# A reordered step table and one copy on another engine, in a fused attention and MLP kernel

## The chip, the cores and the metric

The kernel runs on one NeuronCore of a Trainium2 chip. Its time is the device time of one execution in microseconds (us). Five engines work beside each other, each through its own queue in order: TensorE (PE; its weight loads are shown as PEld), VectorE (DVE), ScalarE (ACT), GpSimd (POOL) and SyncE (SP). DMAs are issued from POOL, SP and ACT, and are carried by 16 DMA engines.

## The reference

Linear attention with decay (4 batches, 8 heads, 768 tokens, head size 64) and behind it an MLP with the activation h + sin(alpha h)^2 / alpha (512 to 2048 to 512). Cut to what is computed:

```python
for b in range(nb):                                   # blocks of 64 tokens
    intra = einsum('bhic,bhjc->bhij', qb, kb) * Dmask
    intra = einsum('bhij,bhjd->bhid', intra, vb)
    inter = einsum('bhid,bhde->bhie', qb * lam_pow, kv_state)
    out[:, :, sl] = intra + inter
    kv_state = lam_block * kv_state + einsum('bhsd,bhse->bhde', kb * rev_pow, vb)
x = out.transpose(0, 2, 1, 3).reshape(B * S, H * D)   # 3072 x 512
h = x @ w_in
s = sin(alpha * h)
g = h + s * s / (alpha + 1e-09)
return g @ w_out
```

## The kernel before

**Tiling.** The 768 tokens are cut into six chunks of 128 (t or g = 0 to 5); a chunk holds these tokens of all four batches, 512 columns. Per chunk the attention gives xt, 512 features x 512 tokens, and the MLP then runs over 16 blocks f of 128 hidden features and, for the output, over four batches m. Matmuls are bf16 into PSUM, which has eight banks of 128 x 512 f32.

**Order.** The first chunk's attention and the tables are written out in plain code. All that follows is one table, the string `ORDER` at the top: 652 words, each a step, issued in exactly this order by the loop at the end through the dictionary `STEP`. An engine runs its own steps in the table's order; between engines only data and buffers make it wait. `h1.4:7` is step h for chunk 1, block 4, in PSUM bank 7. The letters:

- TensorE: `h` the hidden block (four matmuls of 512 columns, L325), `u g.m.part` a quarter of the output projection (four matmuls, L352; part p needs blocks 4p to 4p+3 finished), `F` scores for two batches (four banks, L256), `K` new state from k and v (two banks, L276), `O` attention output (carried part L297, inside part L304, four banks), `e` the last projection in two pieces, 384 and 128 columns (L368).
- ScalarE: `s` sine out of the h bank (L330), `q` its square (L336), `B` cast of the state (L289), `o` copy of an output bank, with the store issued from SP (L358, L360).
- VectorE: `t` finish, which reads the square and the h bank, writes gall and so frees the bank (L345); `Q` and `P` are the square on VectorE, as a tensor_tensor (L338) or a scalar_tensor_tensor (L340); `m` mask of scores (L262), `x` scaling of the attention output (L313), `k` and `j` the transposes of raw k and raw q (L246), `S` the state's update (L285; on ScalarE for chunk 0).
- GpSimd: `I`, `W` loads of w_in and w_out, `r`, `R` of raw k and raw q (four issues each, L123), `n`, `v` of k and v as they lie (two issues each, L130), `d` the decay of k in place (L267), `C` a cast of the state.

A block's chain is thus h, s, q (or Q, P), t, and then the bank is free. Raw k and raw q have one buffer each, so r of the next chunk waits for both k steps of the last; nat_k and nat_v have two. A load from GpSimd's queue also waits until the eighth load ahead of it has landed.

**Where the change acts.** The table's stretch from chunk 1 to chunk 3 is quoted below. The copy that changes is L372 in `project_pieces`, which is the step `e`, the last word of the table:

Of the kernel before, what the change touches and what calls it, by code (L numbers as in the profile page):

```python
# [13 lines left out]


ORDER = """
s0.0 s0.1 I1 h0.4:4 h0.6:5 P0.0 P0.1 t0.0 s0.2 t0.1 s0.3 s0.4 q0.2 q0.3 q0.4 h0.7:6 I2 t0.2 t0.3 d0.1 I3 t0.4
h0.5:2 s0.5 s0.6 s0.7 P0.5 h0.11:3 t0.5 h0.9:1 W0 q0.6 q0.7 t0.6 t0.7 h0.8:0 s0.8 r1 P0.8 t0.8 h0.10:4 h0.12:2
W1 s0.9 s0.10 h0.14:6 u0.1.0:5 R1 q0.9 t0.9 q0.10 t0.10 s0.11 s0.12 h0.13:7 k1.1 u0.2.0:1 q0.11 t0.11 h0.15:4
u0.0.0:0 k1.0 q0.12 t0.12 u0.2.1 s0.13 s0.14 W2 u0.3.0:3 W3 q0.13 t0.13 s0.15 d0.0 K0:72 q0.14 t0.14 v1 u0.1.1  # L20
q0.15 t0.15 S0.0 j1.0 u0.3.1 j1.1 S0.1 F1.0:4627 C0.1 m1.0.1 u0.3.2 u0.2.2 R2 m1.0.0 m1.0.2 u0.1.2 C0.0 m1.0.3
F1.1:7462 u0.0.1 u0.1.3 o0.1 m1.1.2 u0.3.3 o0.3 m1.1.1 m1.1.3 m1.1.0 O1:7562 x1.0 x1.1 u0.0.2 u0.2.3 u0.0.3 o0.0
x1.3 x1.2 h1.0:7 h1.1:0 j2.0 r2 k2.0 h1.2:2 o0.2 s1.0 s1.1 Q1.0 t1.0 q1.1 t1.1 s1.2 h1.3:4 F2.0:6135 m2.0.2 s1.3
m2.0.1 h1.4:7 q1.2 q1.3 t1.2 n1 s1.4 m2.0.0 h1.5:0 s1.5 k2.1 m2.0.3 n2 q1.4 t1.4 h1.6:1 s1.6 q1.5 d1.1 h1.7:2
s1.7 t1.3 h1.8:6 q1.6 t1.6 h1.11:3 t1.5 s1.8 q1.7 q1.8 h1.9:5 h1.10:4 s1.9 s1.10 t1.7 t1.8 u1.0.0:1 h1.12:7 j2.1
h1.13:2 q1.9 t1.9 q1.10 s1.11 t1.10 u1.0.1 d1.0 K1:06 q1.11 t1.11 h1.14:5 u1.2.0:3 v2 S1.0 d2.1 S1.1 d2.0 K2:40
u1.2.1 s1.12 q1.12 s1.13 q1.13 h1.15:6 t1.12 t1.13 S2.0 u1.0.2 s1.14 R3 q1.14 t1.14 r3 s1.15 F2.1:4572 q1.15
S2.1 t1.15 u1.2.2 m2.1.0 B2.0 u1.1.0:0 n3 B1.0 m2.1.2 m2.1.1 B1.1 u1.0.3 u1.2.3 o1.2 B2.1 m2.1.3 O2:5672 j3.0
u1.1.1 u1.1.2 k3.0 x2.0 x2.1 o1.0 x2.3 x2.2 F3.0:4156 m3.0.0 u1.1.3 o1.1 h2.0:7 s2.0 m3.0.1 h2.1:2 k3.1 q2.0
s2.1 q2.1 j3.1 m3.0.2 h2.2:0 s2.2 v3 d3.0 u1.3.0:1 h2.3:4 u1.3.1 q2.2 t2.0 t2.1 t2.2 s2.3 d3.1 F3.1:3257 m3.1.1  # L30
m3.1.2 m3.0.3 u1.3.2 q2.3 K3:02 S3.1 h2.4:5 S3.0 m3.1.3 m3.1.0 R4 s2.4 q2.4 h2.5:6 h2.6:2 s2.5 s2.6 q2.5 t2.3
t2.5 u1.3.3 q2.6 t2.6 j4.0 r4 h2.7:0 s2.7 o1.3 h2.10:4 q2.7 t2.7 h2.8:7 s2.8 n4 O3:2613 t2.4 h2.9:0 x3.0 x3.2
h2.13:5 q2.8 s2.9 x3.3 s2.10 d4.1 d4.0 v4 v5 h2.11:2 x3.1 u2.0.0:1 q2.9 h2.12:6 t2.8 t2.9 u2.0.1 q2.10 t2.10
h3.0:3 s2.11 q2.11 t2.11 k4.0 s2.12 q2.12 t2.12 u2.0.2 s2.13 q2.13 F4.0:4207 m4.0.0 m4.0.2 t2.13 m4.0.1 B3.0
h2.14:6 s2.14 u2.3.0:4 q2.14 h2.15:0 s2.15 q2.15 u2.3.1 t2.14 k4.1 r5 h3.2:5 m4.0.3 s3.0 q3.0 t2.15 j4.1 R5 t3.0
h3.1:6 s3.1 q3.1 s3.2 h3.3:2 t3.1 u2.0.3 u2.1.0:7 q3.2 t3.2 s3.3 h3.4:0 q3.3 t3.3 u2.1.1 u2.3.2 o2.0 s3.4 q3.4
t3.4 u2.1.2 F4.1:6315 m4.1.3 B3.1 u2.3.3 o2.3 m4.1.1 u2.1.3 o2.1 m4.1.0 m4.1.2 u2.2.0:2 O4:1365 h3.5:4 s3.5
h3.6:0 x4.0 u3.1.0:7 x4.1 h3.8:1 s3.6 x4.2 q3.5 t3.5 q3.6 k5.0 h3.7:6 u2.2.1 x4.3 t3.6 s3.7 q3.7 s3.8 u3.0.0:3
u2.2.2 q3.8 h3.9:5 s3.9 q3.9 h3.10:4 s3.10 q3.10 t3.7 j5.1 j5.0 t3.8 u3.0.1 h3.11:0 K4:16 u2.2.3 t3.9 t3.10 S4.1
S4.0 s3.11 q3.11 t3.11 o2.2 u3.1.1 h3.12:1 F5.0:6042 h3.13:5 m5.0.0 u3.1.2 m5.0.3 m5.0.1 h4.0:6 h3.14:0 B4.0  # L40
s3.12 q3.12 s3.13 m5.0.2 q3.13 t3.13 t3.12 B4.1 h3.15:2 u3.2.0:1 h4.1:5 u3.2.1 u3.0.2 u3.2.2 s3.14 q3.14 s3.15
q3.15 t3.14 t3.15 u3.1.3 s4.0 q4.0 t4.0 s4.1 q4.1 o3.1 t4.1 h4.2:0 u3.0.3 o3.0 k5.1 F5.1:6542 m5.1.0 m5.1.2
h4.3:7 m5.1.3 u3.2.3 u3.3.0:6 h4.4:3 s4.2 q4.2 t4.2 m5.1.1 s4.3 q4.3 t4.3 u3.3.1 O5:4072 u3.3.2 x5.0 x5.2 x5.3
o3.2 x5.1 s4.4 q4.4 t4.4 h4.5:5 s4.5 q4.5 t4.5 u3.3.3 o3.3 h4.6:7 s4.6 q4.6 h4.8:0 t4.6 h4.7:2 s4.7 s4.8
u4.0.0:5 q4.7 t4.7 q4.8 h4.9:6 s4.9 q4.9 t4.9 h4.10:1 s4.10 h4.11:7 s4.11 q4.10 q4.11 h5.2:2 h4.12:3 s4.12 t4.8
q4.12 u4.0.1 u4.2.0:6 t4.11 h4.13:0 t4.12 h4.14:7 s4.13 q4.13 t4.13 h4.15:4 s4.14 s4.15 h5.0:3 t4.10 u4.3.0:0
s5.0 u4.0.2 q4.14 u4.2.1 q4.15 q5.0 u4.3.1 h5.1:1 s5.1 q5.1 t4.14 t4.15 u4.0.3 s5.2 q5.2 t5.0 t5.2 h5.3:4 s5.3
u4.3.2 h5.6:7 o4.0 q5.3 t5.1 u4.3.3 o4.3 h5.4:2 s5.4 q5.4 h5.5:5 s5.5 q5.5 t5.3 h5.8:3 t5.4 t5.5 s5.6 h5.7:0
s5.7 q5.6 t5.6 q5.7 s5.8 q5.8 h5.9:2 s5.9 q5.9 u4.2.2 t5.7 u5.0.0:5 u5.1.0:1 u4.2.3 o4.2 t5.9 h5.10:4 s5.10
q5.10 t5.10 h5.13:0 u5.1.1 u5.2.0:2 h5.11:6 s5.11 h5.12:4 s5.12 t5.8 q5.11 q5.12 s5.13 q5.13 t5.11 h5.14:3  # L50
u5.2.1 s5.14 h5.15:7 s5.15 q5.14 u5.2.2 u5.0.1 u5.1.2 t5.12 t5.13 t5.14 u4.1.0:4 u5.0.2 q5.15 t5.15 u5.1.3
u5.2.3 o5.1 u5.0.3 o5.0 o5.2 u4.1.1 u4.1.2 u4.1.3 o4.1 e5.3:60
"""


# [1 line left out]
def kernel(  # L57
# [304 lines left out]
    def project_pieces(g, m, *bks):  # L362
        row = m * S + g * T
        for bk, cols in zip(bks, (slice(0, 384), slice(384, DM))):
            w = cols.stop - cols.start
            ps = bank("ops", bk)
            for f in range(NFC):
                nc.tensor.matmul(out=ps[:, 0:w], lhsT=gall[g][:, f, m * P:(m + 1) * P],  # L368
                                 rhs=w_out_sb[f // 4][:, f % 4, cols],
                                 start=(f == 0), stop=(f == NFC - 1))  # L370
# [1 line left out]
            A.copy(out=o_sb[:, 0:w], in_=ps[:, 0:w])  # L372
# [182 lines left out]
```

## Time and profile before

| | |
|---|---|
| median of 3 runs | 208.8 us (208.12 to 209.15) |
| profiled execution | 207.95 us, span 206.2 |
| TensorE, share of the span | 97% |
| VectorE, ScalarE | 69%, 69% |
| GpSimd | 39%, its last load issued at 110 us |
| h and u matmuls, 368 each | 86.5 and 87.5 us |
| squares on ScalarE | 91 of 96, 55.6 us, 635 ns each |
| squares on VectorE | 4 at 687 ns (L340), 1 at 414 ns (L338) |
| masks, finishes, transposes on VectorE | 685, 741 and some 1110 ns each |
| decay of k on GpSimd | 10 at 1904 ns |

The span is the time from the first to the last event of the profiled execution; the rest of its time lies around it. A line of the profile's order of time gives start and length in us, engine, line of the kernel, operation, output and inputs, the count of instructions merged and, in brackets, the engine's idle time ahead of it and what ended it. Matmul ends are modelled and overlap the next start.

### The profile page before, as it was taken

How to read it: one execution, taken by the hardware profiler on the slowest of the kernel's cores; microseconds unless marked ns; L12 is line 12 of the kernel's file. 1: busy time of each engine (PE TensorE's matmuls, PEld its weight loads, DVE VectorE, ACT ScalarE, POOL GpSimd, SP SyncE). 2: the span in 40 equal slices, each digit the busy share in tenths (PEclk: the TensorE clock that was granted, in tenths of full speed). 3: DMA queues.
4: the chain of work that ended last, by engine and by line, in shares of the span. 5: the costliest groups of instructions: out<-in, count | busy, mean ns of one | idle time of the engine just before them, and what ended most of it. 6: DMA issues, size and time to landing. Idle time of an engine off the chain costs nothing.

```text
span 206.2 us, 4975 instructions
## 1 busy us (share of the span) xinstructions
PE 200.3 (97%) x2068; PEld 104.8 (51%) x2068; DVE 142.2 (69%) x212; ACT 142.7 (69%) x251; POOL 80.5 (39%) x103
## 2 busy tenths in 40 slices
...
GB/s 123 166 178 203 208 204 209 177 193 219 211 26 95 150 163 233 131 168 80 66 149 166 183 5 3 54 0 51 102 3 51 3 0 34 69 51 0 3 153 102
DMA packets 63808, 22.61 MB, mean 110 GB/s; under 512 B 46758, under 2 KB 60326, under 8 KB 63786
## 3 DMA queue, kind: packets, MB, share of 16 engines
...
q14 instruction: 6, 0.05, 0.1%
...
## 4 chain that ended last, share of the span: by engine, by line
PE 61%; POOL 17%; DMA 17%; issue 2%; DVE 1%; ACT 0%; POOLq 0%; DVEq 0%; ACTq 0%
PE ops L352 27%; PE hps L325 27%; POOL nat_k L267 5%; DMA nat_v<-in_v_dram 5%; DMA nat_k<-in_k_dram 5%; DMA w_out<-in_moe_w_out_dram 4%; POOL raw_q L123 3%; POOL w_in L139 3%; POOL nat_v L130 3%; DMA raw_k<-in_k_dram 3%; PE ops L368 2%; PE F_ps L256 2%; PE O_ps L304 1%; POOL nat_k L130 1%; PE O_ps L297 1%
## 5 line engine op out<-in xcount | busy, mean ns | idle before, releaser
L345 DVE SCALAR_TENSOR_TENSOR gall<-s,r_sb,hps 128x512 bf16<-128x512 bf16 x96 | 68.3, 741 | 31.2 <-ACT s L336 31.0
L352 PE MATMUL ops<-w_out,gall 128*128 128x512 bf16 x368 | 87.5, 379 | 0.0
L325 PE MATMUL hps<-xt,w_in 128*128 128x512 bf16 x368 | 86.5, 380 | 0.5 <-DVE gall L345 0.4
L330 ACT ACTIVATE s_sb<-hps,alpha_sb 128x512 bf16<-128x512 f32 x96 | 63.7, 687 | 24.3 <-PE hps L325 23.3
L325 PEld LDWEIGHTS <-w_in 128*128 128x128 bf16 x368 | 40.9, 114 | 38.0 <-issue 0.7
L336 ACT ACTIVATE s<-s_sb 128x512 bf16<-128x512 bf16 x91 | 55.6, 635 | 1.6
L352 PEld LDWEIGHTS <-gall 128*128 128x128 bf16 x368 | 35.0, 98 | 41.1
L262 DVE TENSOR_TENSOR STm<-F_ps,C 128x512 bf16<-128x512 f32 x48 | 30.3, 685 | 4.8 <-PE F_ps L256 4.6
L358 ACT COPY o_sb<-ops 128x512 f32<-128x512 f32 x23 | 13.3, 584 | 26.1 <-PE ops L352 25.9
L267 POOL TENSOR_TENSOR nat_k<-nat_k,R 128x1024 bf16<-128x1024 bf16 x10 | 18.9, 1904 | 14.3 <-DMA nat_k<-in_k_dram 14.3
L123 POOL DMA_DIRECT2D raw_q<-in_q_dram x24 | 14.2, 597 | 6.8 <-DVE turned_q L246 3.1
L313 DVE TENSOR_TENSOR xt<-O_ps,Etab 128x512 bf16<-128x512 f32 x20 | 12.5, 682 | 4.2 <-PE O_ps L304 4.2
L246 DVE STREAM_TRANSPOSE turned_q<-raw_q 128x512 f32<-128x512 f32 x12 | 12.8, 1109 | 2.1 <-DMA raw_q<-in_q_dram 1.9
L130 POOL DMA_DIRECT2D nat_v<-in_v_dram x12 | 14.0, 1174 | 0.0
L246 DVE STREAM_TRANSPOSE turned_k<-raw_k 128x512 f32<-128x512 f32 x10 | 11.2, 1116 | 3.2 <-DMA raw_k<-in_k_dram 3.2
L123 POOL DMA_DIRECT2D raw_k<-in_k_dram x20 | 11.5, 584 | 4.5 <-DVE turned_k L246 3.1
L130 POOL DMA_DIRECT2D nat_k<-in_k_dram x9 | 10.6, 1189 | 0.0
L256 PEld LDWEIGHTS <-turned_k 32*128 32x128 bf16 x384 | 6.0, 94 | 6.1 <-issue 3.1
L186 PE MATMUL spare<-fill 128*128 128x512 bf16 x18 | 7.5, 534 | 1.5 <-DVE one L167 1.5
L256 PE MATMUL F_ps<-turned_q,turned_k 32*128 32x128 bf16 x384 | 8.2, 218 | 0.3 <-DVE turned_k L246 0.2
...
L285 DVE SCALAR_TENSOR_TENSOR S<-S,L,KV_ps 128x512 f32<-128x512 f32 x8 | 5.7, 747 | 0.0
...
## 6 DMA issues: line engine op xcount, KB each, us to landing
...
```

Source lines behind the costliest of these rows:

```text
L123: (eng or G).dma_start(out=dst[quad[a], bs].rearrange("t b n r d -> t (b n) (r d)"), in_=src[t, a])
L130: G.dma_start(out=nat[nm, t][:, bs].rearrange("p b h e -> p (b h) e"), in_=SRC[nm][bs, :, t * T:(t + 1) * T, :].rearrange("b h p e -> p (b ...
L246: V.transpose(out=dst.rearrange("p (x t r) -> p x r t", r=R, t=32), in_=src.rearrange("p (x r d) -> p x r d", r=R, d=32))
L256: nc.tensor.matmul(out=F[a][:, u, n, :], lhsT=kt[:, :, e] if t else kt[:, e, :], rhs=KQ["q", t][quad[a], 2 * pr + u, n, :, e], start=(e == ...
L262: V.tensor_tensor(out=st[t, pr][:, a], in0=att["F", pr][a], in1=(C0 if t else C1)[:, a].unsqueeze(1).broadcast_to([P, 2, NQ, T]), op=ALU.mult)
L267: G.tensor_tensor(out=kd, in0=kd, in1=R128[:].unsqueeze(1).unsqueeze(3).broadcast_to([P, 2, H, D]), op=ALU.mult)
L325: nc.tensor.matmul(out=hps[g, f][:], lhsT=w_in_block(f, c), rhs=xt[g][:, c, :], start=(c == 0), stop=(c == NDC - 1))
L330: A.activation(out=s_of[g, f][:], in_=hps[g, f][:], func=ACTF.Sin, scale=alpha_sb[:, f:f + 1])
L336: A.activation(out=s2_of[g, f][:], in_=s_sb[:], func=ACTF.Square)
L345: V.scalar_tensor_tensor(out=gall[g][:, f, :], in0=s2_of.pop((g, f))[:], scalar=r_sb[:, f:f + 1], in1=hps.pop((g, f))[:], op0=ALU.mult, op ...
L352: nc.tensor.matmul(out=ops[g, m][:], lhsT=gall[g][:, f, m * P:(m + 1) * P], rhs=w_out_sb[part][:, f % 4, :], start=(f == 0), stop=(f == NF ...
L358: A.copy(out=o_sb[:], in_=ops.pop((g, m))[:])
```

## The change

Two edits. The table holds the same number of words, with loads, matmuls and banks in another order; 26 squares that were `q` are now `Q` (14 more than before) or `P` (12 more). And the second piece of the last step is copied by VectorE.

```diff
@@ project_pieces @@
-            A.copy(out=o_sb[:, 0:w], in_=ps[:, 0:w])
+            if cols.stop < DM:
+                A.copy(out=o_sb[:, 0:w], in_=ps[:, 0:w])
+            else:
+                V.tensor_copy(out=o_sb[:, 0:w], in_=ps[:, 0:w])
@@ ORDER @@
...
-u0.0.0:0 k1.0 q0.12 t0.12 u0.2.1 s0.13 s0.14 W2 u0.3.0:3 W3 q0.13 t0.13 s0.15 d0.0 K0:72 q0.14 t0.14 v1 u0.1.1
-q0.15 t0.15 S0.0 j1.0 u0.3.1 j1.1 S0.1 F1.0:4627 C0.1 m1.0.1 u0.3.2 u0.2.2 R2 m1.0.0 m1.0.2 u0.1.2 C0.0 m1.0.3
-F1.1:7462 u0.0.1 u0.1.3 o0.1 m1.1.2 u0.3.3 o0.3 m1.1.1 m1.1.3 m1.1.0 O1:7562 x1.0 x1.1 u0.0.2 u0.2.3 u0.0.3 o0.0
-x1.3 x1.2 h1.0:7 h1.1:0 j2.0 r2 k2.0 h1.2:2 o0.2 s1.0 s1.1 Q1.0 t1.0 q1.1 t1.1 s1.2 h1.3:4 F2.0:6135 m2.0.2 s1.3
-m2.0.1 h1.4:7 q1.2 q1.3 t1.2 n1 s1.4 m2.0.0 h1.5:0 s1.5 k2.1 m2.0.3 n2 q1.4 t1.4 h1.6:1 s1.6 q1.5 d1.1 h1.7:2
-s1.7 t1.3 h1.8:6 q1.6 t1.6 h1.11:3 t1.5 s1.8 q1.7 q1.8 h1.9:5 h1.10:4 s1.9 s1.10 t1.7 t1.8 u1.0.0:1 h1.12:7 j2.1
-h1.13:2 q1.9 t1.9 q1.10 s1.11 t1.10 u1.0.1 d1.0 K1:06 q1.11 t1.11 h1.14:5 u1.2.0:3 v2 S1.0 d2.1 S1.1 d2.0 K2:40
-u1.2.1 s1.12 q1.12 s1.13 q1.13 h1.15:6 t1.12 t1.13 S2.0 u1.0.2 s1.14 R3 q1.14 t1.14 r3 s1.15 F2.1:4572 q1.15
-S2.1 t1.15 u1.2.2 m2.1.0 B2.0 u1.1.0:0 n3 B1.0 m2.1.2 m2.1.1 B1.1 u1.0.3 u1.2.3 o1.2 B2.1 m2.1.3 O2:5672 j3.0
-u1.1.1 u1.1.2 k3.0 x2.0 x2.1 o1.0 x2.3 x2.2 F3.0:4156 m3.0.0 u1.1.3 o1.1 h2.0:7 s2.0 m3.0.1 h2.1:2 k3.1 q2.0
-s2.1 q2.1 j3.1 m3.0.2 h2.2:0 s2.2 v3 d3.0 u1.3.0:1 h2.3:4 u1.3.1 q2.2 t2.0 t2.1 t2.2 s2.3 d3.1 F3.1:3257 m3.1.1
-m3.1.2 m3.0.3 u1.3.2 q2.3 K3:02 S3.1 h2.4:5 S3.0 m3.1.3 m3.1.0 R4 s2.4 q2.4 h2.5:6 h2.6:2 s2.5 s2.6 q2.5 t2.3
-t2.5 u1.3.3 q2.6 t2.6 j4.0 r4 h2.7:0 s2.7 o1.3 h2.10:4 q2.7 t2.7 h2.8:7 s2.8 n4 O3:2613 t2.4 h2.9:0 x3.0 x3.2
...
+u0.0.1 m1.1.1 O1:7254 u0.0.2 u0.2.3 x1.0 x1.3 u0.0.3 r2
+o0.3 n1 n2 x1.1 x1.2 h1.0:7 v2 o0.0 h1.1:0 o0.2 h1.2:2 j2.0 j2.1 k2.0 s1.0 q1.0 s1.1 q1.1 t1.0 t1.1 h1.3:4
+F2.0:5136 d1.1 m2.0.1 h1.4:7 s1.2 s1.3 d1.0 q1.2 q1.3 m2.0.3 h1.5:0 s1.4 t1.2 s1.5 h1.6:1 s1.6 t1.3 m2.0.2
+m2.0.0 h1.7:6 q1.4 t1.4 h1.10:4 h1.8:2 q1.5 t1.5 q1.6 t1.6 s1.7 h1.9:5 h1.12:7 s1.8 d2.1 h1.11:0 k2.1 q1.7 t1.7
+s1.9 q1.8 t1.8 d2.0 q1.9 u1.0.0:1 t1.9 K1:36 S1.0 u1.0.1 s1.10 s1.11 q1.10 q1.11 t1.10 t1.11 s1.12 q1.12 h1.13:2
+s1.13 S1.1 u1.2.0:3 h1.14:5 s1.14 t1.12 K2:40 S2.0 h1.15:6 q1.13 q1.14 t1.13 t1.14 s1.15 u1.0.2 B1.1 R3 S2.1
+q1.15 t1.15 u1.2.1 B1.0 F2.1:7425 m2.1.0 u1.2.2 u1.1.0:0 u1.0.3 u1.2.3 o1.2 m2.1.2 m2.1.3 o1.0 m2.1.1 O2:6257
+j3.0 u1.1.1 u1.1.2 B2.0 r3 k3.0 x2.0 x2.1 F3.0:3216 n3 d3.1 v3 n4 u1.1.3 o1.1 x2.3 x2.2 h2.0:5 m3.0.2 h2.1:7
+m3.0.1 j3.1 u1.3.0:1 s2.0 q2.0 s2.1 h2.2:0 q2.1 k3.1 m3.0.0 s2.2 u1.3.1 t2.0 t2.1 q2.2 t2.2 h2.3:4 s2.3 q2.3
+F3.1:3257 m3.1.1 d3.0 B2.1 m3.1.2 u1.3.2 K3:02 m3.0.3 h2.4:5 s2.4 q2.4 m3.1.3 h2.5:6 m3.1.0 s2.5 t2.3 h2.8:7
+t2.4 R4 h2.6:3 S3.0 S3.1 q2.5 s2.6 u1.3.3 t2.5 h2.7:5 q2.6 t2.6 d4.0 o1.3 h2.9:0 s2.7 s2.8 j4.0 h2.10:4 q2.7
...
```

GpSimd's steps in the table, before:

```text
I1 I2 d0.1 I3 W0 r1 W1 R1 W2 W3 d0.0 v1 C0.1 R2 C0.0 r2 n1 n2 d1.1 d1.0 v2 d2.1 d2.0 R3 r3 n3 v3 d3.0 d3.1 R4 r4 n4 d4.1 d4.0 v4 v5 r5 R5
```

and after:

```text
I1 I2 d0.1 I3 W0 r1 W1 R1 W2 d0.0 W3 C0.0 v1 C0.1 R2 r2 n1 n2 v2 d1.1 d1.0 d2.1 d2.0 R3 r3 n3 d3.1 v3 n4 d3.0 R4 d4.0 r4 v4 v5 r5 d4.1 R5
```

TensorE's first steps are `h0.4 h0.6 h0.7 h0.5 h0.11 h0.9 h0.8 h0.10 h0.12 h0.14 u0.1.0` before, and `h0.4 h0.5 h0.6 h0.8 h0.7 h0.10 h0.9 h0.11 h0.12 u0.1.0` after. In chunks 4 and 5 the banks that the prediction names lie in this order on TensorE after the change: `h4.2:2 u3.1.3 h4.4:4 h4.3:3 F5.1:2507`, `h4.5:7 u3.3.1 O5:1253 h4.9:7` and `h5.0:7 u4.2.1 h5.2:2 h5.6:4 h5.3:7`; and the last words of the table are `u4.1.3 o4.1 e5.3:23` where they were `u4.1.3 o4.1 e5.3:60`.

More of the change, by code (lines that the diff above doesn't have):

```diff
@@ L16 @@
 ORDER = """
-s0.0 s0.1 I1 h0.4:4 h0.6:5 P0.0 P0.1 t0.0 s0.2 t0.1 s0.3 s0.4 q0.2 q0.3 q0.4 h0.7:6 I2 t0.2 t0.3 d0.1 I3 t0.4
-h0.5:2 s0.5 s0.6 s0.7 P0.5 h0.11:3 t0.5 h0.9:1 W0 q0.6 q0.7 t0.6 t0.7 h0.8:0 s0.8 r1 P0.8 t0.8 h0.10:4 h0.12:2
-W1 s0.9 s0.10 h0.14:6 u0.1.0:5 R1 q0.9 t0.9 q0.10 t0.10 s0.11 s0.12 h0.13:7 k1.1 u0.2.0:1 q0.11 t0.11 h0.15:4
-u0.0.0:0 k1.0 q0.12 t0.12 u0.2.1 s0.13 s0.14 W2 u0.3.0:3 W3 q0.13 t0.13 s0.15 d0.0 K0:72 q0.14 t0.14 v1 u0.1.1
-q0.15 t0.15 S0.0 j1.0 u0.3.1 j1.1 S0.1 F1.0:4627 C0.1 m1.0.1 u0.3.2 u0.2.2 R2 m1.0.0 m1.0.2 u0.1.2 C0.0 m1.0.3
@@ L32 @@
-t2.5 u1.3.3 q2.6 t2.6 j4.0 r4 h2.7:0 s2.7 o1.3 h2.10:4 q2.7 t2.7 h2.8:7 s2.8 n4 O3:2613 t2.4 h2.9:0 x3.0 x3.2
[L33 to L51, printed above, removed]
@@ L52 @@
-u5.2.3 o5.1 u5.0.3 o5.0 o5.2 u4.1.1 u4.1.2 u4.1.3 o4.1 e5.3:60
+I1 s0.0 P0.0 t0.0 I2 h0.4:7 s0.1 s0.2 P0.1 h0.5:4 s0.3 h0.6:5 h0.8:6 t0.1 h0.7:3 q0.2 P0.3 s0.4 s0.5 t0.2 t0.3
+h0.10:0 q0.4 t0.4 s0.6 q0.5 P0.6 t0.5 t0.6 h0.9:1 s0.7 s0.8 h0.11:7 d0.1 I3 h0.12:2 q0.7 t0.7 q0.8 s0.9 s0.10
+t0.8 W0 r1 u0.1.0:5 q0.9 t0.9 h0.13:4 q0.10 t0.10 k1.0 s0.11 s0.12 s0.13 W1 R1 k1.1 u0.3.0:3 q0.11 q0.12 W2
+t0.12 q0.13 t0.13 u0.2.0:1 h0.14:0 s0.14 h0.15:6 u0.2.1 s0.15 u0.1.1 t0.11 q0.14 q0.15 t0.14 t0.15 d0.0 K0:74 W3
@@ new lines @@
+S0.0 j1.0 S0.1 C0.0 v1 u0.3.1 u0.0.0:0 F1.0:7264 u0.2.2 C0.1 j1.1 m1.0.1 m1.0.2 m1.0.0 m1.0.3 u0.1.2 u0.3.2
+F1.1:7264 m1.1.3 m1.1.0 m1.1.2 u0.3.3 u0.1.3 o0.1 R2 u0.0.1 m1.1.1 O1:7254 u0.0.2 u0.2.3 x1.0 x1.3 u0.0.3 r2
+o0.3 n1 n2 x1.1 x1.2 h1.0:7 v2 o0.0 h1.1:0 o0.2 h1.2:2 j2.0 j2.1 k2.0 s1.0 q1.0 s1.1 q1.1 t1.0 t1.1 h1.3:4
+F2.0:5136 d1.1 m2.0.1 h1.4:7 s1.2 s1.3 d1.0 q1.2 q1.3 m2.0.3 h1.5:0 s1.4 t1.2 s1.5 h1.6:1 s1.6 t1.3 m2.0.2
+m2.0.0 h1.7:6 q1.4 t1.4 h1.10:4 h1.8:2 q1.5 t1.5 q1.6 t1.6 s1.7 h1.9:5 h1.12:7 s1.8 d2.1 h1.11:0 k2.1 q1.7 t1.7
@@ new lines @@
+F3.1:3257 m3.1.1 d3.0 B2.1 m3.1.2 u1.3.2 K3:02 m3.0.3 h2.4:5 s2.4 q2.4 m3.1.3 h2.5:6 m3.1.0 s2.5 t2.3 h2.8:7
+t2.4 R4 h2.6:3 S3.0 S3.1 q2.5 s2.6 u1.3.3 t2.5 h2.7:5 q2.6 t2.6 d4.0 o1.3 h2.9:0 s2.7 s2.8 j4.0 h2.10:4 q2.7
+t2.7 r4 q2.8 t2.8 O3:1263 x3.0 x3.3 s2.9 q2.9 s2.10 x3.2 q2.10 t2.10 h2.13:5 x3.1 h2.11:7 s2.11 u2.0.0:1 h2.12:6
+t2.9 q2.11 t2.11 s2.12 s2.13 k4.0 u2.0.1 h3.0:3 q2.12 t2.12 u2.0.2 F4.0:4207 m4.0.0 h2.14:6 m4.0.2 m4.0.3
+u2.3.0:4 m4.0.1 q2.13 s2.14 Q2.14 h2.15:0 t2.13 s2.15 Q2.15 t2.14 B3.0 u2.1.0:7 k4.1 h3.1:2 v4 h3.3:5 B3.1
```

17 lines of the change are left out of this document (added).

## The prediction

> **What bounds the kernel now.** I read the page first, its engine shares and slices, then TensorE's order of time, then what VectorE and GpSimd did at the places where TensorE waited.
>
> ```profile
> span 206.2 us, 4975 instructions
> PE 200.3 (97%) x2068; PEld 104.8 (51%) x2068; DVE 142.2 (69%) x212; ACT 142.7 (69%) x251; POOL 80.5 (39%) x103
> ```
>
> TensorE is busy 97% of the span, every other engine at most 69%. The change alters no matmul: both tables hold 92 h, 92 u, 10 F, 5 K and 5 O steps. So only time in which TensorE stands can be won. I price its steps by the distance from start to start where nothing waits: an h or u 0.864 us (four matmuls of 216 ns), F 0.57, K 0.62, O 1.70, and 0.10 more for whatever stands ahead of an F, K or O. From the first h at 19.82 that is 184 x 0.864 + 10 x 0.67 + 5 x 0.72 + 5 x 1.80 = 178.3, so the last step, e5.3, would start at 198.1. It starts at 199.48. **All standing in the table's part is 1.4 us**, 0.7% of the span. Nearly all of it is at two places. TensorE at the first:
>
> ```profile
> 47.95 3.62 PE L325 MATMUL hps<-xt,w_in 128*128 128x512 bf16 x16
> 51.77 0.64 PE L256 MATMUL F_ps<-turned_q,turned_k 32*128 32x128 bf16 x32 [0.20 <-DVE turned_k L246]
> 52.81 5.51 PE L325 MATMUL hps<-xt,w_in 128*128 128x512 bf16 x24 [0.39 <-DVE gall L345]
> ```
>
> Columns: start, length, engine, line, operation, tiles, count, and the wait before with what ended it. Four h from 47.95 take 3.46, plus 0.10: F2.0 was due at 51.51 and starts at 51.77, 0.27 late. h1.4 was due 0.57 later, at 52.34, and starts at 52.81, 0.46 late. The six h steps behind it lose 0.16 more (5.51 against 6 x 0.864 and 0.16 of drain). VectorE over the same time:
>
> ```profile
> 50.60 1.11 DVE L246 STREAM_TRANSPOSE turned_k<-raw_k 128x512 f32<-128x512 f32 x1 [2.31 <-DMA raw_k<-in_k_dram]
> 51.56 0.41 DVE L338 TENSOR_TENSOR s<-s_sb 128x512 bf16<-128x512 bf16 x1
> 52.01 1.41 DVE L345 SCALAR_TENSOR_TENSOR gall<-s,r_sb,hps 128x512 bf16<-128x512 bf16 x2
> 53.33 1.28 DVE L262 TENSOR_TENSOR STm<-F_ps,C 128x512 bf16<-128x512 f32 x2
> ```
>
> The transpose k2.0 stood 2.31 us for the third chunk's raw k. Queued behind it are the square Q1.0 and then t1.0, t1.1, and t1.0 frees bank 7, which h1.4 needs. The second place, TensorE and then VectorE:
>
> ```profile
> 76.88 0.90 PE L256 MATMUL F_ps<-turned_q,turned_k 32*128 32x128 bf16 x32
> 77.72 1.04 PE L352 MATMUL ops<-w_out,gall 128*128 128x512 bf16 x4
> ```
>
> ```profile
> 74.90 1.10 DVE L246 STREAM_TRANSPOSE turned_k<-raw_k 128x512 f32<-128x512 f32 x1 [0.90 <-DMA raw_k<-in_k_dram]
> 75.85 2.46 DVE L313 TENSOR_TENSOR xt<-O_ps,Etab 128x512 bf16<-128x512 f32 x4
> ```
>
> F3.0 takes 0.84 to the next step instead of 0.57: k3.0 waited for raw k until 74.77, the x2 steps came behind it, and F3.0 needs the banks that they free. That is 0.27. The rest is 0.07 ahead of O1 and six inherent 0.03s. Sum: 0.27 + 0.46 + 0.16 + 0.27 + 0.07 + 0.16 = 1.4.
>
> **The change part by part.** *h1.4 and the third chunk.* TensorE meets the same steps up to h1.6. On VectorE the order becomes j2.0 j2.1 k2.0 t1.0 t1.1: j2.1 (1.10) lies in the 2.31 us wait, and Q1.0 is gone, its square being on ScalarE (q1.0), which has t1.0's input ready before 51.5. If raw k lands at its 50.5 again, k2.0 ends at 51.7, F2.0 keeps its 0.27, t1.0 runs 51.55 to 52.3 (0.45 earlier) and h1.4, due at 52.34, no longer waits. The m steps behind end 0.46 earlier too. Removed: 0.46 + 0.16.
>
> *GpSimd from 55 us on.* Its order of time now:
>
> ```profile
> 55.41 3.76 POOL L267 TENSOR_TENSOR nat_k<-nat_k,R 128x1024 bf16<-128x1024 bf16 x2 [6.14 <-DMA nat_k<-in_k_dram]
> 59.11 2.35 POOL L130 DMA_DIRECT2D nat_v<-in_v_dram  x2
> 61.48 3.78 POOL L267 TENSOR_TENSOR nat_k<-nat_k,R 128x1024 bf16<-128x1024 bf16 x2
> 65.19 2.35 POOL L123 DMA_DIRECT2D raw_q<-in_q_dram  x4
> 67.53 2.29 POOL L123 DMA_DIRECT2D raw_k<-in_k_dram  x4
> 69.82 2.31 POOL L130 DMA_DIRECT2D nat_k<-in_k_dram  x2
> 72.11 2.30 POOL L130 DMA_DIRECT2D nat_v<-in_v_dram  x2
> 76.60 3.76 POOL L267 TENSOR_TENSOR nat_k<-nat_k,R 128x1024 bf16<-128x1024 bf16 x2 [2.19 <-DMA nat_k<-in_k_dram]
> ```
>
> v2 (the 2.35 at 59.11) goes ahead of d1.1, into the 6.14 us in which GpSimd stands. What follows d1.0 comes 2.3 us earlier: d2 59.2 to 62.95, R3 from 62.95, r3 from 65.3, n3 67.6 to 69.9. Raw k of the fourth chunk, landing 9.58 after R3's first issue as before (65.19 to 74.77), is there at 72.5, so k3.0 and x2.0, x2.1 end ahead of F3.0. Removed: 0.27. R3 needs j2.1 done, and that now ends near 49; r3 needs k2.1, near 59.7.
>
> *What is added: K3.* Before, n3 and v3 were issued back to back and d3.0, d3.1 came last. Now the order is n3 d3.1 v3 n4 d3.0 R4. d3.1 waits for n3's second half; behind it on GpSimd's queue stand v3, n4 and d3.0, and K3 on TensorE waits for v3 and d3.0. n3's issues took 6.7 and 7.4 to landing: 67.6 + 6.7 = 74.3, 68.75 + 7.4 = 76.15. Then d3.1 to 78.1, v3 to 80.35, n4 to 82.65, d3.0 to 84.55. K3 is due at 85.41 less 0.9, 84.5. v3's second half, issued at 79.2, lands 5.8 later at 85.0 if it goes like v2 at 59.11 (63.9 and 66.1), and K3's second half, due at 84.85, needs it. I take **0.3 added**, by the nearest row, v2's. The ends: nothing, and 2.3, if n3's second half lands at 78.39 as before. Then R4, some 2.8 later than before, ends close to j4.0 (both near 91.2), and t2.7 still has 0.9 before h2.13 needs bank 5.
>
> *The other moved loads.* C0.0 now stands ahead of v1, and C0.1 behind it, so v1 is issued at 36.6 instead of 32.0 and R2 perhaps 0.7 later. The DMA slices read 9 tenths through 41 us and landings follow one another (w_out's last at 40.06, v1 41.8 and 43.8), so a later issue lands the same while the line is not empty. I take nothing; 0.7 is the far end, and it would go straight onto F2.0. W3 moves behind d0.0 (1.9): it lands at 40.06 in line, its first user is due at 40.88. h0.8, the first user of the third w_in tile, goes from fifth to fourth, due at 22.41 against a landing at 22.20; u0.1.0 at 27.6 against 27.25. Nothing, at most 0.2 each.
>
> *Squares.* 26 of ScalarE's squares (635 ns each, 16.5 us, all beside TensorE) go to VectorE: 14 more as Q (414 ns) and 12 more as P (687 ns), 14.0 us. By stage VectorE was busy 16.7 of 22 us (98 to 120), 16.6 of 22, 9.2 of 14 and 15.6 of 34. With the squares, and with two transposes of 1.1 moved from the second stage to the first, these become 21.5, 18, 10.5 and 23: the first is tight. The queue there is followed step by step from these rows: the smallest spares are h5.0 to h5.3 on bank 7 (0.15), h4.2 to F5.1 on bank 2 (0.25), h4.5 to h4.9 on bank 7 (0.35). Before, h4.13 ended at 163.38 with bank 0 reused at 165.81, 2.4 later, without a wait; h5.0 to h5.3 has the same 2.4. Nothing, from -0.1 to 0.8 if several of them miss.
>
> *The last copy.* It is on the path whole:
>
> ```profile
> 202.32 0.48 ACT L372 COPY o_sb<-ops 128x384 f32<-128x384 f32 x1 [2.01 <-PE ops L368]
> 203.22 0.27 ACT L372 COPY o_sb<-ops 128x128 f32<-128x128 f32 x1 [0.41 <-PE ops L368]
> ```
>
> ScalarE has been idle 0.41 when the piece is ready, so nothing is unblocked. VectorE read 256 columns from PSUM in 425 ns and 512 in 685, a slope that gives some 295 for 128; the ends are 207 (128 columns from SBUF) and 425. Against 267 that is -0.06 to +0.16, and I take zero. [...]
>
> **Sum**: -0.62 - 0.27 + 0.3 = **-0.6 us**. The profiled execution took 207.95 with a span of 206.2, so its like would be 207.35 with 205.6. Its median over the runs is 208.8, 0.85 higher, and I carry the difference over: **208.2**.
>
> **The rivals.** *B, slower: d3.1 holds GpSimd.* If n3's second half lands at 78.39 instead of 76.15, v3, n4 and d3.0 follow at once, d3.0 ends near 86.9, and TensorE stands 2.3 us at K3: -0.9 + 2.3 = +1.4, 210.2. It turns to a loss from a landing at 77.1 on. For it: the stores o1.2 and o1.0 were under way while n3 landed, and took up to 6.6 us; v3's first half then came 4 us behind n3. Against it: n3's halves came 1.75 and 1.87 apart beside these stores, hardly slower than n2's 1.6. [...] Chance 0.17.
>
> *C, no change: the loads of the third chunk slip.* v1 and R2 are issued later, raw k lands up to 0.7 later, and F2.0 and h1.4 lose what was won: 208.8 with K3's wait at nothing. The line of DMAs without gaps speaks against it. Chance 0.13.
>
> *D, VectorE's queue.* Where squares stand ahead of a t or an m, banks come late at three or more of the places above, 0.3 to 0.8 together: 208.5 to 209.5. VectorE's spare time by stage speaks against it. Chance 0.10.
>
> **How the numbers follow.** The forecast has 0.60; its own range is 207.6 (F2.0's wait gone as well and none at K3) to 208.7. This kernel's runs, 208.12 to 209.15, tell some 0.5% from no change, about 1.0 us. More than 1.0 faster needs nearly all of the 1.4 back: 0.15. Slower by over 1.0: 0.13 of B, 0.05 of D, 0.02 of C, 0.20 together. Between: 0.65. The range runs from 207.5 to 209.9, most of the way to B.
>
> **What would show it.** Right: h1.4 starts 0.57 behind F2.0; F3.0 takes 0.57; K3 starts within 0.5 us of 84.5, d3.0 ending just ahead; the last step starts at 198.6 to 199.1. Wrong: raw k's transpose k2.0 beginning after 50.9; d3.1 beginning after 77; waits of TensorE on gall or STm beyond 100 us.

## The result, and the profile after

| | before | after |
|---|---|---|
| median of 11 runs | 208.48 us (207.81 to 209.37) | 209.59 us (209.0 to 211.12) |
| profiled execution, span | 207.95, 206.2 | 210.09, 208.4 |
| first h to e5.3, start to start | 179.66 | 182.12 |
| of it TensorE standing (less 178.28) | 1.39 | 3.84 |

The ratio after to before is 1.0062 with an interval of 1.0037 to 1.0088: the change made the kernel slower, by some 1.3 us, where 0.6 us of gain had been forecast. The direction is wrong. That the time still lies inside the range is luck: the upper end was drawn for rival B, and the larger part of the loss came from a term that was set at nothing. The profiled execution of after lies 0.5 above its median and that of before 0.5 below, so the two traces together show 2.1 us of difference, more than the medians' 1.1. The traces tell where time goes; the ratios tell how much.

The head of the page of after:

```profile
span 208.4 us, 4991 instructions
PE 199.3 (96%) x2068; PEld 104.7 (50%) x2068; DVE 153.8 (74%) x239; ACT 127.2 (61%) x224; POOL 80.5 (39%) x103
```

ScalarE is busy 15.5 us less and VectorE 11.6 more, the moved squares. TensorE's matmuls are the same 2068, and only its standing grew. Laid out step by step as in the prediction, 1.99 of the 3.84 stand at F2.0, 1.20 at K3, 0.24 at h2.13, 0.22 around F1.0, 0.11 at u2.2.0, and no other place beyond 100 us holds more than 0.03. TensorE's order of time at the first two:

```profile
47.77 3.62 PE L325 MATMUL hps<-xt,w_in 128*128 128x512 bf16 x16
53.30 0.64 PE L256 MATMUL F_ps<-turned_q,turned_k 32*128 32x128 bf16 x32 [1.92 <-DVE turned_k L246]
...
77.85 0.64 PE L256 MATMUL F_ps<-turned_q,turned_k 32*128 32x128 bf16 x32
78.42 1.04 PE L352 MATMUL ops<-w_out,gall 128*128 128x512 bf16 x4
86.11 0.42 PE L276 MATMUL KV_ps<-nat_v,nat_k 128*32 128x64 bf16 x32
87.58 0.42 PE L276 MATMUL KV_ps<-nat_v,nat_k 128*32 128x64 bf16 x32 [1.05 <-DMA nat_v<-in_v_dram]
```

F2.0 was due at 51.32 and starts at 53.30. F3.0 takes 0.57 to the next step, as forecast. K3's second half waits for the fourth chunk's v. VectorE ahead of F2.0:

```profile
47.08 2.07 DVE L246 STREAM_TRANSPOSE turned_q<-raw_q 128x512 f32<-128x512 f32 x2
52.16 1.09 DVE L246 STREAM_TRANSPOSE turned_k<-raw_k 128x512 f32<-128x512 f32 x1 [3.01 <-DMA raw_k<-in_k_dram]
53.11 0.67 DVE L345 SCALAR_TENSOR_TENSOR gall<-s,r_sb,hps 128x512 bf16<-128x512 bf16 x1
```

j2.1 lies in the wait, as planned (two transposes from 47.08), and t1.0 follows at once, without a square ahead of it. But k2.0 starts at 52.16 instead of 50.60, still waiting for raw k of the third chunk. GpSimd's order of time tells why that load is late. First before, then after:

```profile
31.99 2.37 POOL L130 DMA_DIRECT2D nat_v<-in_v_dram  x2
36.43 0.60 POOL L289 CAST Sb<-S 128x512 bf16<-128x512 f32 x1 [2.08 <-ACT S L283]
```

```profile
35.60 0.61 POOL L289 CAST Sb<-S 128x512 bf16<-128x512 f32 x1 [4.03 <-ACT S L283]
36.15 2.31 POOL L130 DMA_DIRECT2D nat_v<-in_v_dram  x2
39.00 2.30 POOL L123 DMA_DIRECT2D raw_q<-in_q_dram  x4
...
44.31 0.58 POOL L123 DMA_DIRECT2D raw_k<-in_k_dram  x1 [1.30 <-DMA nat_v<-in_v_dram]
```

C0.0 needs S0.0 from ScalarE, and GpSimd, which runs its steps in order, stood 4.03 us for it with v1 behind it. Before, v1's issues began at 31.99, ahead of both casts. The raw loads behind were issued at nearly the same times in both (the first of raw q at 38.76 and 39.00, the last of raw k at 44.12 and 44.31). From windows of 2 us, columns: stretch and length, busy time and count on PE, PEld, DVE, ACT, POOL, then granted clock, DMA share (the packets' time as a mean share of the 16 engines; packets overlap, and it passes 1 here), GB/s. First before, then after:

```profile
38.00:40.00 2.00, 2.00 (x12) 0.88 (x9) 2.00 (x4) 0.00 (x0) 1.24 (x3) 1.00 2.05 163
40.00:42.00 2.00, 2.00 (x40) 1.00 (x39) 1.18 (x3) 0.00 (x0) 2.00 (x4) 1.00 2.39 167
```

```profile
38.00:40.00 2.00, 2.00 (x11) 0.81 (x9) 2.00 (x4) 0.00 (x0) 2.00 (x4) 1.00 1.43 119
40.00:42.00 2.00, 2.00 (x40) 1.07 (x39) 1.08 (x3) 0.00 (x0) 2.00 (x5) 1.00 2.28 144
```

The DMA line ran thin: 163 GB/s became 119, 167 became 144, while the share in the thin window still reads 1.43. Over the five windows from 36 to 46 the differences (-3, 44, 23, 7 and 18 GB/s, times 2 us) come to 178 KB that had not been carried. The landings, read from the transfers: v1 itself lands within 0.2 us of before (41.64 and 44.03 against 41.82 and 43.83), but the raw loads behind it land later, the last of raw k at 52.04 instead of 50.48.

GpSimd at the second place:

```profile
60.53 3.76 POOL L267 TENSOR_TENSOR nat_k<-nat_k,R 128x1024 bf16<-128x1024 bf16 x2 [0.53 <-DMA nat_k<-in_k_dram]
...
68.84 2.34 POOL L130 DMA_DIRECT2D nat_k<-in_k_dram  x2
77.58 1.90 POOL L267 TENSOR_TENSOR nat_k<-nat_k,R 128x1024 bf16<-128x1024 bf16 x1 [6.40 <-DMA nat_k<-in_k_dram]
79.44 2.35 POOL L130 DMA_DIRECT2D nat_v<-in_v_dram  x2
81.77 2.30 POOL L130 DMA_DIRECT2D nat_k<-in_k_dram  x2
84.06 1.95 POOL L267 TENSOR_TENSOR nat_k<-nat_k,R 128x1024 bf16<-128x1024 bf16 x1
```

The same pattern: d3.1 stands 6.40 us for n3's second half (landed 77.51) and v3 stands behind it. v3's second half, issued at 80.63, lands at 87.54, and K3's second half starts at 87.58. The last copy:

```profile
205.34 0.29 DVE L375 COPY o_sb<-ops 128x128 f32<-128x128 f32 x1 [13.07 <-PE ops L368]
```

It takes 291 ns where ScalarE's took 267.

### The profile page after: what moved, and what is told of

Its sections match the earlier page's. It is cut to its first block, busy times and chain, and to the rows that moved or that the text cites. A ratio compares the mean times of both kernels' runs of the same rounds, so it can differ in the third digit from the quotient of the medians.

```text
span 208.4 us, 4991 instructions
## 1 busy us (share of the span) xinstructions
PE 199.3 (96%) x2068; PEld 104.7 (50%) x2068; DVE 153.8 (74%) x239; ACT 127.2 (61%) x224; POOL 80.5 (39%) x103
## 4 chain that ended last, share of the span: by engine, by line
PE 62%; DMA 19%; POOL 14%; issue 2%; DVE 1%; ACT 0%; POOLq 0%; DVEq 0%
PE hps L325 27%; PE ops L352 27%; DMA nat_k<-in_k_dram 8%; DMA nat_v<-in_v_dram 7%; POOL nat_k L267 5%; DMA raw_q<-in_q_dram 4%; POOL raw_q L123 3%; POOL nat_k L130 3%; PE hps L462 2%; POOL nat_v L130 2%; PE ops L368 2%; POOL raw_k L123 1%; PE F_ps L256 1%; PE O_ps L304 1%; PE O_ps L297 1%
## 5 line engine op out<-in xcount | busy, mean ns | idle before, releaser
L325 PE MATMUL hps<-xt,w_in 128*128 128x512 bf16 x368 | 86.5, 380 | 0.2 <-DVE gall L345 0.2
L325 PEld LDWEIGHTS <-w_in 128*128 128x128 bf16 x368 | 41.1, 114 | 37.2 <-issue 0.2
L336 ACT ACTIVATE s<-s_sb 128x512 bf16<-128x512 bf16 x65 | 39.8, 643 | 0.9
L123 POOL DMA_DIRECT2D raw_k<-in_k_dram x20 | 11.6, 591 | 11.8 <-DVE turned_k L246 10.2
L340 DVE SCALAR_TENSOR_TENSOR s<-s_sb 128x512 bf16<-128x512 bf16 x16 | 11.0, 686 | 1.7 <-ACT s_sb L330 1.7
L186 PE MATMUL spare<-fill 128*128 128x512 bf16 x18 | 6.9, 500 | 1.5 <-DVE one L167 1.5
```

What stands on the lines that cost most here:

```text
L123: (eng or G).dma_start(out=dst[quad[a], bs].rearrange("t b n r d -> t (b n) (r d)"), in_=src[t, a])
L325: nc.tensor.matmul(out=hps[g, f][:], lhsT=w_in_block(f, c), rhs=xt[g][:, c, :], start=(c == 0), stop=(c == NDC - 1))
L336: A.activation(out=s2_of[g, f][:], in_=s_sb[:], func=ACTF.Square)
```

## The experiments

**Theory 1** (taken up after the result): a step on GpSimd's queue that waits for another engine holds the loads behind it. C0.0 ahead of v1 costs F2.0 its 1.7 us, and d3.1 ahead of v3 costs K3 its 1.2. **Theory 2**: the loads were issued in time enough, and R2 and r2 landed late because the stores o0.1 and o0.3 ran beside them (issued at 43.30 and 43.79, landed at 50.82 and 51.77, before at 48.74 and 49.86). **Theory 3**: the squares on VectorE cost time as well. Standing is always worked out as in the table above, from the first h to e5.3. In the kernels of these runs all lines have numbers one higher (L326 for L325).

**One load back ahead of the cast** (a1_v1_first), after with

```diff
-W3 S0.0 j1.0 S0.1 C0.0 v1 u0.3.1
+W3 v1 S0.0 j1.0 S0.1 C0.0 u0.3.1
```

> The changed kernel with the two loads v1 issued right behind W3, ahead of C0.0. Theory 1 (GpSimd stands 4.0 us at C0.0 with v1 behind it, the DMA line thins near 38 us and every load of the third chunk slips): raw k of the third chunk lands near 50.5 instead of 52.04, F2.0's wait falls from 1.99 us to about 0.3, h1.4 does not wait; K3's wait stays between 0.8 and 1.5. Time about 1.6 us below the changed kernel, near 208.0, ratio to before 0.998. Theory 2 (the stores o0.1 and o0.3, issued 0.5 us apart instead of 0.86, take the DMA time from raw k): F2.0's wait stays above 1.4 us and the ratio above 1.004.

Measured: 1.0006 (0.998 to 1.0033) against before. GpSimd and one window of this kernel:

```profile
31.57 2.32 POOL L131 DMA_DIRECT2D nat_v<-in_v_dram  x2
35.63 1.16 POOL L290 CAST Sb<-S 128x512 bf16<-128x512 f32 x2 [1.75 <-ACT S L284]
```

```profile
38.00:40.00 2.00, 2.00 (x11) 0.78 (x8) 1.97 (x4) 0.00 (x0) 1.38 (x3) 1.00 2.09 162
```

The line carries as much as before again (162 GB/s against 163), raw k lands at 50.28, and F2.0 waits 0.31 instead of 1.99. The stores o0.1 and o0.3 are issued as close together as in after (at 43.23 and 43.72) and land at 48.55 and 49.55, so theory 2 falls here. K3 still stands 0.66, less than the 0.8 that was expected.

**The other load back ahead of the decay** (a2_v3_first), after with

```diff
-n3 d3.1 v3 n4
+n3 v3 d3.1 n4
```

> The changed kernel with v3 issued right behind n3, ahead of d3.1. Theory 3 (v3 is late only because it stands behind d3.1's wait for n3): v3's second half lands near 83 instead of 87.5, K3's wait falls from 1.2 us to below 0.2, and d3.0 ends earlier than 86.0 too; F2.0's wait of 2.0 stays. Time about 1.2 us below the changed kernel, near 208.4, ratio to before 1.000. Rival (K3 waits for d3.0 behind n4 anyway): K3 still waits 0.5 or more, ratio above 1.003.

Measured: 1.0007 (0.9985 to 1.0028). GpSimd and TensorE of this kernel:

```profile
68.32 2.32 POOL L131 DMA_DIRECT2D nat_k<-in_k_dram  x2
70.62 2.31 POOL L131 DMA_DIRECT2D nat_v<-in_v_dram  x2
77.94 1.90 POOL L268 TENSOR_TENSOR nat_k<-nat_k,R 128x1024 bf16<-128x1024 bf16 x1 [5.01 <-DMA nat_k<-in_k_dram]
```

```profile
85.77 0.69 PE L277 MATMUL KV_ps<-nat_v,nat_k 128*32 128x64 bf16 x64
86.39 3.65 PE L326 MATMUL hps<-xt,w_in 128*128 128x512 bf16 x16
```

GpSimd still stands 5.01 us at d3.1, but v3's issues are now ahead of that wait: v3's second half lands at 82.39 instead of 87.54, and both halves of K3 run through. F2.0 keeps 1.60 here.

**Both** (a3_both), the two edits together.

> The changed kernel with both moves. If both theories hold and the two waits are independent: F2.0's wait about 0.3, K3's below 0.2, all standing in the table's part 0.9 us or less against 1.39 before and 3.84 after: time near 207.6, ratio to before 0.996. If one wait takes the other's place: ratio at or above 1.000.

Measured: 0.9968 (0.9945 to 0.999), standing 1.00, nothing at K3. F2.0 still stands 0.61 late in this execution, more than the 0.3 that was expected:

```profile
52.20 0.64 PE L257 MATMUL F_ps<-turned_q,turned_k 32*128 32x128 bf16 x32 [0.55 <-DVE turned_k L247]
```

Two words moved in the table, and the loss of 0.6% has become a gain of 0.3%. Each word alone gives back some 0.0055, both together 0.0094; within the intervals the two add up.

**The suspected harm put into before** (b1_v1_late): the cast C0.1, for which GpSimd waits, goes ahead of v1, and nothing else changes.

```diff
-q0.14 t0.14 v1 u0.1.1
+q0.14 t0.14 u0.1.1
...
-F1.0:4627 C0.1 m1.0.1
+F1.0:4627 C0.1 v1 m1.0.1
```

> The kernel before with nothing but v1 moved behind C0.1, where GpSimd stands for S0.1. Theory 1: the DMA line thins as in the changed kernel, raw k of the third chunk lands 1.5 to 2 us later than 50.48, F2.0's wait grows from 0.27 to 1.8 or more; time 1.2 to 2.0 us above before, ratio 1.006 to 1.010. Theory 2 (the stores): raw k lands within 0.4 of 50.48 and the ratio is within 0.002 of 1.

Measured: 1.0101 (1.0051 to 1.0151). The window of this kernel:

```profile
38.00:40.00 2.00, 2.00 (x11) 0.88 (x9) 2.00 (x4) 0.00 (x0) 2.00 (x4) 1.00 0.96 87
```

87 GB/s, raw k's last at 53.23, F2.0 standing 2.02, and also O1, which here loses 1.04 us, mostly to v1 itself. So the harm can be made from before with one word.

Not all of the 6.1 us that this trace stands is waiting. Behind F2.0 TensorE's granted clock (third column from the right) fell:

```profile
54.00:56.00 2.00, 1.11 (x34) 0.80 (x35) 1.96 (x4) 1.47 (x3) 0.00 (x0) 0.96 1.87 207
56.00:58.00 2.00, 2.00 (x6) 0.73 (x5) 2.00 (x5) 0.69 (x1) 0.52 (x1) 0.50 1.93 229
58.00:60.00 2.00, 2.00 (x7) 0.78 (x6) 2.00 (x3) 1.14 (x2) 2.00 (x2) 0.68 1.39 89
```

The windows before and behind have 1.00, and the steps from h1.4 to h1.6 take 1.7 us longer than their price. Of this kernel's six runs, three have a mean clock of 0.990 to 0.992 and take 211.12 to 212.23 us; the other three, at 0.997 to 1.000, take 209.28 to 209.64, some 1.1 us more than before's median of 208.34. So, as far as these clocks tell, the ratio of 1.0101 mixes the price of the loads, about 0.005 and near the 0.0056 of a1, with that of the clock. In after's trace, where F2.0 waits almost as long (1.92 in the view against 1.96 here), the clock stays at 1.00; what decides between the two, no run here shows.

**h1.4 freed of the load** (c1_h14_first), a3 with t1.0 ahead of the transpose and h1.4 ahead of F2.0:

```diff
-h1.1:0 o0.2 h1.2:2 j2.0 j2.1 k2.0 s1.0 q1.0 s1.1 q1.1 t1.0 t1.1 h1.3:4 F2.0:5136 d1.1 m2.0.1 h1.4:7
+h1.1:0 h1.2:2 s1.0 q1.0 o0.2 j2.0 j2.1 t1.0 k2.0 s1.1 q1.1 t1.1 h1.3:4 h1.4:7 F2.0:5136 d1.1 m2.0.1
```

> The version with both loads moved (a3), and at F2.0: t1.0 ahead of k2.0 on VectorE, h1.4 ahead of F2.0 on TensorE, s1.0 and q1.0 ahead of the copy o0.2 on ScalarE. If what is left at F2.0 (0.61 us in a3) is the landing of raw k alone, F2.0 comes 0.86 later and its wait goes to 0.1 or less: standing in the table's part 0.5 us, time 0.4 to 0.6 below a3, near 207.1, ratio to before 0.994. Rival (t1.0's chain s1.0, q1.0 is too late for h1.4, or o0.2 comes too late for F2.0's bank 1): the wait moves to h1.4 or F2.0 and the time stays at a3's, ratio 0.997.

Measured: 0.994 (0.9908 to 0.9973), 207.21 us, standing 0.1. TensorE:

```profile
47.94 4.48 PE L326 MATMUL hps<-xt,w_in 128*128 128x512 bf16 x20
52.35 0.64 PE L257 MATMUL F_ps<-turned_q,turned_k 32*128 32x128 bf16 x32
```

Five h and then F2.0 on its due time, as also in d1 below. Against a3's 0.9968 the intervals overlap, so the further gain is seen in the trace and not settled in the time.

**The last copy back on ScalarE** (c2_scalar_copy, on a3; d1_best, on c1):

```diff
-            if cols.stop < DM:
-                A.copy(out=o_sb[:, 0:w], in_=ps[:, 0:w])
-            else:
-                V.tensor_copy(out=o_sb[:, 0:w], in_=ps[:, 0:w])
+            A.copy(out=o_sb[:, 0:w], in_=ps[:, 0:w])
```

> a3 with the last copy back on ScalarE. The time from the start of the last step to the end of the span, 6.76 to 6.84 us in the four runs with VectorE's copy, against 6.72 and 6.74 with ScalarE's, becomes 6.70 to 6.75; the total cannot be told from a3's, ratio to before 0.995 to 0.999. Rival (the copy on VectorE helps): 6.85 or more.

> The version with both loads moved and h1.4 ahead of F2.0 (c1), with the last copy on ScalarE. Standing in the table's part 0.5 us or less, as in c1: ratio to before 0.992 to 0.995. If c1's profile was a lucky draw of the loads: 0.997.

Measured: 0.9934 (0.9906 to 0.9961) and 0.995 (0.9924 to 0.9975), against 0.9968 and 0.994 with VectorE: no difference that the times can tell, though c2's ratio lies below the 0.995 to 0.999 expected. From the start of e5.3 to the end of the span it is 6.75 to 6.76 us in three traces with ScalarE (before, c2, d1) and 6.79 in the six with VectorE, 0.04 more; the expectation's 6.72 to 6.84 came from spans rounded to 0.1 us, which is coarser than the difference. d1's trace stands 0.80, more than the 0.5 expected, 0.5 of it ahead of u0.1.0 near 28 us, where w_out was awaited. The three versions c1, c2 and d1 beat both kernels by their medians, 207.2 to 207.8 us, and can't be told apart.

**The squares** (c3_squares_back: a3 with 27 squares of chunks 2 to 5 as `q` on ScalarE, in the places where they stand; c4_before_squares: before with the same 27 on VectorE). After has moved 29 squares to VectorE and 3 back, the 26 net; 27 of the 29 lie in chunks 2 to 5. For example

```diff
@@ a3 to c3 @@
-s3.14 s3.15 Q3.13 P3.14 P3.15 t3.14 t3.13
+s3.14 s3.15 q3.13 q3.14 q3.15 t3.14 t3.13
@@ before to c4 @@
-q3.12 s3.13 m5.0.2 q3.13 t3.13 t3.12
+Q3.12 s3.13 m5.0.2 Q3.13 t3.13 t3.12
```

> a3 with the 27 squares of chunks 2 to 5 that stand on VectorE back on ScalarE, in their places in the table. If the squares cost nothing and bring nothing, ScalarE's 17 us more lie beside TensorE: standing within 0.3 us of a3's 1.0, ratio to before within 0.002 of a3's 0.9968. If VectorE's squares are what keeps chunks 3 to 5 free of waits: waits of TensorE on gall or STm appear beyond 100 us, 0.5 us or more in sum, and the ratio is above 0.999.

> The kernel before with nothing but the same 27 squares on VectorE. If VectorE's queue is no bound (prediction's rival D wrong): standing within 0.4 us of 1.39, ratio to before within 0.003 of 1. If it is: waits on gall or STm beyond 100 us, standing 2 us or more, ratio above 1.003.

Measured: c3 1.005 (1.0024 to 1.0075), c4 1.0286 (1.0222 to 1.035). A line of TensorE of c3, and then two of c4:

```profile
168.74 1.02 PE L326 MATMUL hps<-xt,w_in 128*128 128x512 bf16 x4 [1.04 <-DVE gall L346]
```

```profile
131.23 0.39 PE L353 MATMUL ops<-w_out,gall 128*128 128x512 bf16 x1 [1.89 <-DVE gall L346]
...
133.68 0.69 PE L277 MATMUL KV_ps<-nat_v,nat_k 128*32 128x64 bf16 x64 [1.20 <-DVE gall L346]
```

In c3 the waits on gall (1.2 at h5.3 and 0.3 at 158 us) make some 1.5 us; the rest of its 3.2 us of standing is mostly loads in this execution (O1 1.1, F2.0 0.57). In c4 there are six waits on gall beyond 100 us, 3.9 us together in the view and 4.8 laid out step by step. So the squares go with the table that was made for them: in it they cost nothing, in before's table 2.9%, and taken out of the new table they cost some 0.8% as well. Theory 3 falls for the change as made.

**The parts that should gain, alone** (b2_gain_parts), before with

```diff
-h1.1:0 j2.0 r2 k2.0 h1.2:2 o0.2 s1.0 s1.1 Q1.0 t1.0
+h1.1:0 j2.0 j2.1 r2 k2.0 h1.2:2 o0.2 s1.0 s1.1 q1.0 t1.0
...
-m2.0.3 n2 q1.4 t1.4
+m2.0.3 n2 v2 q1.4 t1.4
...
-h1.12:7 j2.1 h1.13:2
+h1.12:7 h1.13:2
...
-u1.2.0:3 v2 S1.0
+u1.2.0:3 S1.0
```

> The kernel before with the three moves that the prediction counted as gains and nothing else: j2.1 ahead of k2.0, Q1.0 back on ScalarE as q1.0, v2 ahead of d1.1. If the prediction's gain was sized right: no wait at h1.4 and h1.6, none inside F3.0, standing in the table's part lower by 0.8 to 0.9 us, ratio to before 0.995 to 0.997. Rival (the gain is taken back at F2.0 or K3): ratio 0.999 or more.

Measured: 0.9977 (0.9953 to 1.0002), 207.94 us, standing 0.40. The trace shows the waits at h1.4 and F3.0 gone, and F2.0 standing 0.29 as in before (0.27), which the prediction had kept; the time falls just short of what was expected, and its interval reaches no change. Likely a gain, not shown.

**The decay ahead of v3 in before** (b3_d31_first, repeated as b3_again):

```diff
-n3 B1.0 m2.1.2
+n3 d3.1 v3 n4 d3.0 B1.0 m2.1.2
```

with d3.1, v3, n4 and d3.0 taken out of their old places.

> The kernel before with nothing but GpSimd's order n3 d3.1 v3 n4 d3.0 of the changed kernel. If d3.1's wait for n3 delays v3 and d3.0 by itself: d3.1 begins near 78.5, v3 is issued near 80.3 and lands near 88, K3, due at 85.4, waits 1.5 to 3 us; time 1.5 to 3 us above before, ratio 1.007 to 1.014. If K3's wait needs the late loads of the third chunk too: K3 waits under 0.5, ratio within 0.002 of 1.

> The kernel before with nothing but GpSimd's order n3 d3.1 v3 n4 d3.0, a second time, for a profile at the full clock. If d3.1's wait alone delays K3: d3.1 begins near 78.5 to 80, d3.0 ends 6 us later and K3 waits for it 2 to 3 us; ratio to before 1.010 to 1.018 as the first time (1.0153).

Measured: 1.0153 (1.0094 to 1.0211) and 1.012 (1.0068 to 1.0171). Both profiled executions hold a stretch at half clock, behind the longest wait of each, so that their mean granted clocks are 0.984 and 0.990; the second trace is read here. Its TensorE:

```profile
85.80 0.42 PE L277 MATMUL KV_ps<-nat_v,nat_k 128*32 128x64 bf16 x32 [0.62 <-POOL nat_k L268]
86.53 0.42 PE L277 MATMUL KV_ps<-nat_v,nat_k 128*32 128x64 bf16 x32 [0.31 <-DMA nat_v<-in_v_dram]
...
97.15 2.08 PE L326 MATMUL hps<-xt,w_in 128*128 128x512 bf16 x6 [2.33 <-DVE gall L346]
```

K3 waits 0.93, for d3.0 and then v3, less than the 1.5 to 3 that were expected. The larger part is one step further: R4 stands behind all of it on GpSimd's queue, lands at 95.36, and j4.0, which waits for it on VectorE, holds the finishes that free the banks behind O3: 2.33. Behind that wait the granted clock is 0.50 from 98 to 100 us, and three steps lose another 1.7. The three runs of the repeat at a clock of 1.00 took 210.1 to 211.05 us against 208.07 for before, so most of the loss is there without the slower clock. In after the same chain shows at h2.13 with 0.24.

## Why the prediction was wrong

**The step that failed** is the one on the other moved loads: v1 behind C0.0, of which it said "I take nothing; 0.7 is the far end". It measured 1.72 at F2.0 (1.99 less the 0.27 that was there); of that, 0.2 is TensorE arriving earlier in the profiled execution (due at 51.32, before at 51.51) and 1.5 the landing. k2.0 began at 52.16, past the 50.9 that was named as a sign. One trace does not give the size to a tenth: with v1 early and F2.0 in its old place, nine traces have F2.0 from 0 to 0.96 late, 0.45 in the mean, and the three with v1 behind a cast (after, a2, b1) 1.60 to 2.02. The two groups do not overlap. The ratios say the same: moving v1 alone back gives 0.0056, 1.2 us. The premise "a later issue lands the same while the line is not empty" was not tested by itself, but the reading of the slices was wrong: their digits stop at 9, and the page of after shows the same nines in its DMA slices over these microseconds. With v1 not issued until 36.15 there was too little behind W3, 119 GB/s were carried between 38 and 40 us instead of 163, and v1 caught up while the raw k behind it stayed late. 178 KB at the some 180 GB/s of these windows are 1.0 us; what makes the last raw k another 0.5 later was not settled. The price was to be read from GpSimd's trace of before: it stood 2.08 us at the cast C0.1, and v1, issued ahead of that wait, had been in line all the while.

**Rival C** had this mechanism, late raw k, and too small a price; its chance of 0.13 rested on the same "line of DMAs without gaps".

**K3's term was mis-sized**: 0.3 forecast, 1.20 measured. n3 was issued at 68.84 instead of 67.6, since n1 and n2 were late with the other loads: d1.1 began at 56.24 instead of 55.41, and d2.1 waited 0.53 for n2. n3's second half landed at 77.51 instead of 76.15; and v3's second half took 6.9 us from issue to landing, not 5.8 like v2's. With the third chunk's loads in time (a1) K3 still stands 0.66, so, by these two traces, somewhat over half of the 0.9 that was missed (0.54) goes with the first error, and the rest stays without it. **Rival B** has the right place: n3's second half landed at 77.51, past its turning point of 77.1, and d3.1 began at 77.58, past the mark of 77 that was to show the forecast wrong. But what TensorE waited for in the main was v3 behind d3.1, 1.05, and not d3.0, which ended at 86.01, just ahead of K3 at 86.11; K3 itself came 1.6 later than the 84.5 forecast, mostly by F2.0, which hid that much of the delay. Nor do the stores that rival B had in its favour show in n3's second half: in after o1.2 and o1.0 were issued at 75.03 and 75.53, and n3's halves landed at 75.96 and 77.51, 1.55 us apart, against 1.87 before.

**Right, and shown**: h1.4 no longer waits (0.46) and h1.6 hardly (0.07 at h1.5 in place of 0.16), F3.0's 0.27 is gone, in after and in a3; no wait of weight on VectorE beyond 100 us, so rival D did not happen, though c4 shows that the margin was the table's and not VectorE's spare time. The last copy was estimated at 295 ns and took 291; at the end of the span it costs 0.04, inside the bounds of -0.06 to 0.16.

**The sum, mended**: -0.62 - 0.27 + 1.72 + 1.20 + 0.24 and the small ones (0.22 at F1.0, 0.11 at u2.2.0, less 0.15 in old small ones that are gone) make +2.45, which is the difference of standing in the table, 3.84 - 1.39. The runs' median shows about half of that.
